# Retention and mixture of experts on one core: the value products of four heads are cut to the key halves their queries see

## The chip, the cores and the metric

The kernel runs on one core of a Trainium2 chip. The metric is the device time of one execution in microseconds (us); three timed runs of the kernel before gave a median of 569.94 us (569.82 to 571.11).

## The reference, cut to what matters

Retention over 8 batches, 8 heads, 576 positions and 64 channels, then a mixture of 16 experts (4 groups of 4) over the 4608 tokens. The change lies in the first part, in `ret @ v`:

```python
B, H, S, D_ = q.shape                        # 8, 8, 576, 64
scores = scale * np.matmul(q, k.transpose(0, 1, 3, 2))
rel = pos[:, None] - pos[None, :]
Dmat = np.where(rel >= 0, gamma[:, None, None] ** rel[None, :, :], 0.0)
ret = scores * Dmat[None, :, :, :]
out = np.matmul(ret, v)                      # causal: a query sees no later key
...
# each token: best group, best expert in it, two layers with ReLU, weighted
ye = np.maximum(xg[mask_e] @ w1[g, e], 0.0) @ w2[g, e]
```

All of the retention is in float32.

## The kernel before, in words

The retention runs over 36 tiles of 128 tokens (`NT`), nine to a pair of batches: eight of one batch each (four tiles per batch) and a ninth (`m` is 1) with the last 64 tokens of both. Earlier tiles of a batch act through a running state, so within a tile only 128 keys by 128 queries are left, masked to be causal. The order on TensorE is written out by hand (the loop at L942): everything there runs in program order, and VectorE, ScalarE, GpSimd and SyncE are pinned to program order too.

In step t of that loop TensorE does, one behind the other: `av(t - 1)` (L887), `state(t)` (L866), `inter(t - 1)` (L902), `scores(t + 1)` (L828), the transposes `xnat_pe(t - 6)` (L427) and, once in three steps each, `logits`, `gate_pe`, `places_pe`.

- `scores` makes keys by queries for eight heads in the PSUM tile `pss` (one buffer, one bank for each `o`). A head is named by s, g and o: h = 4s + 2g + o. From tile 5 on, 64 by 64 products that leave late keys by early queries out (L843) make all heads of two thirds of the tiles and half the heads of the others (t % 3 is 1); the other half there, the second tile of each nine and the first five tiles are made whole (L851).
- `masked` (L856) multiplies `pss` by a mask on VectorE into `sT` (two buffers).
- `av` multiplies `sT` with the scaled values `vs` (three buffers, made by ScalarE in `scale`): for each head 128 keys by 128 queries into the PSUM tile `px`, 64 output rows, so two heads (g = 0, 1) stand side by side in the columns of the array.
- `state` adds the tile's keys by values to the running sums `pst`; `inter` adds, for tiles that have a state before them, state by queries to `px` as 64-row products, four at a time. Eight of the 36 tiles, the first of each batch, have no `inter`; the ninth tiles have two half-wide ones and no `state`.
- `turned` (L919) reads `px` on VectorE into `xT`; what follows (gate, rows to DRAM by GpSimd's scatters, experts) builds on that.

To let 64-row products of two heads stand in different rows of the array, the host exchanges the key halves of every second pair of heads (`_layout`, L1554; the decay constants follow at L1512), so that a head's early keys lie in rows 0 to 63 or 64 to 127. The loads of the tiles (`a`, seven buffers, 1 MB each) go out on SyncE's queue, `loads(t + 6)` in step t. The experts follow on TensorE from step 36 on (L1178).

A float32 product is two MATMUL records on TensorE, a bfloat16 or float32r one is one.

## Time and profile before

| | us |
|---|---|
| median of three runs | 569.94 |
| the profiled execution | 569.17 |
| its span, first to last instruction | 567.4 |
| TensorE busy | 556.8 (98% of the span) |
| VectorE busy | 428.1 (75%) |
| ScalarE busy | 329.8 (58%) |
| granted TensorE clock | 0.999 of full speed |

The span is the stretch that the trace covers; 1.8 us of the execution lie outside it. The retention takes TensorE until 143 us, the experts the rest. In the trace's rows a group such as "PE L894 MATMUL px<-sT,vs 128*64 128x128 f32 x16" is 16 MATMUL records of line 894 that write `px` from `sT` and `vs`; 128*64 are the rows and columns of the array that they use, 128x128 the operand that is streamed (128 partitions, 128 columns).

### The profile page before, as it was taken

The page shows a single profiled execution, that of the slowest core. Times are in us where ns is not written, and L with a number is a line of the kernel's source. Part 1 is how long each engine was busy: PE and PEld are TensorE (multiplying, and loading weights), DVE is VectorE, ACT ScalarE, POOL GpSimd, SP SyncE. Part 2 cuts the span into 40 slices and gives each one's busy share as a digit, 9 for nine tenths or more (in the row PEclk, how much of TensorE's full clock was granted, in tenths as well). Part 3 has the DMA queues.
Part 4 walks back from the last instruction along what each step waited for, and adds up shares of the span by engine and source line. Part 5 has one row for each costly group of instructions (what it writes and reads, how often), then busy time and mean ns, then how long its engine had stood idle before and what let it go on. Part 6 is the DMA issues. An engine that isn't in the chain of part 4 may idle for free.

```text
span 567.4 us, 16419 instructions
## 1 busy us (share of the span) xinstructions
PE 556.8 (98%) x6014; PEld 527.1 (93%) x6014; DVE 428.1 (75%) x1007; ACT 329.8 (58%) x855; POOL 265.3 (47%) x400
## 2 busy tenths in 40 slices
PE   7999999999999999999999999999999999999995
PEld 5888888888799999999999999999999999999994
DVE  5887787878899678876768586777768677687784
ACT  5678878886664545454545455554545455555553
POOL 0022323253502056555564758374564836638564
PEclk9999999999999999999999999999999999999999
DMA  8999999979666975655556464928566484754751
GB/s 334 424 393 344 336 365 333 355 245 353 235 226 276 203 310 154 252 158 243 177 221 209 191 230 183 352 67 335 136 261 210 193 293 143 323 199 195 292 222 42
DMA packets 47639, 142.01 MB, mean 250 GB/s; under 512 B 7825, under 2 KB 28697, under 8 KB 34864
## 3 DMA queue, kind: packets, MB, share of 16 engines
q1 hardware_dynamic: 38176, 120.18, 59.1%
q0 software_dynamic: 9216, 20.34, 9.9%
q8 instruction: 72, 1.18, 0.8%
q14 instruction: 31, 0.25, 0.1%
q10 hardware_dynamic: 144, 0.05, 0.0%
HBM read 120.22 MB, written 24.81 MB: 256 GB/s over the span
## 4 chain that ended last, share of the span: by engine, by line
PE 93%; DMA 2%; POOL 1%; SPq 1%; DVE 1%; issue 1%; ACT 0%; POOLq 0%; ACTq 0%
PE ph L691 35%; PE py L1102 11%; PE py L1104 11%; PE py L1103 11%; PE px L894 6%; PE pxt L434 4%; PE pss L843 3%; PE px L913 3%; PE pst L879 2%; PE py L1091 2%; DMA a<-in_qkv 2%; PE plt L484 2%; PE pss L851 1%; POOL out L121 1%; SPq L121 1%; PE phn L1156 1%
## 5 line engine op out<-in xcount | busy, mean ns | idle before, releaser
L121 POOL DMA_INDIRECT out<-y,ii x151 | 165.4, 1095 | 59.5 <-issue 29.7
L121 DVE TENSOR_TENSOR wl<-r,wh 128x512 fp32r<-128x512 f32 x268 | 172.4, 686 | 4.0 <-ACT wh L121 0.8
L121 ACT ACTIVATE hh<-ph 128x256 fp32r<-128x256 f32 (+15 forms) x128 | 53.8, 420 | 187.5 <-PE ph L691 132.5
L121 ACT CAST wh<-r 128x512 fp32r<-128x512 f32 x268 | 151.6, 618 | 0.0
L691 PE MATMUL ph<-xTh_m,wh 128*128 128x316 f32 (+15 forms) x504 | 148.4, 294 | 0.0
L691 PE MATMUL ph<-xTh_m,wl 128*128 128x316 f32 (+15 forms) x504 | 148.0, 294 | 0.0
L691 PE MATMUL ph<-xTl_m,wh 128*128 128x316 f32 (+15 forms) x504 | 147.9, 294 | 0.0
L1102 PE MATMUL py<-hh,wh 128*128 128x316 f32 (+18 forms) x480 | 142.0, 296 | 0.0
L1104 PE MATMUL py<-hl,wh 128*128 128x316 f32 (+13 forms) x480 | 141.1, 294 | 0.0
L1103 PE MATMUL py<-hh,wl 128*128 128x316 f32 (+13 forms) x480 | 141.0, 294 | 0.0
L121 DVE SCALAR_TENSOR_TENSOR hl<-ph,hh 128x256 fp32r<-128x256 f32 (+14 forms) x126 | 58.5, 464 | 87.0 <-ACT hh L121 86.4
L691 PEld LDWEIGHTS ph<-xTh_m,wh 128*128 128x128 f32 x504 | 95.2, 189 | 0.6 <-issue 0.3
L691 PEld LDWEIGHTS ph<-xTl_m,wh 128*128 128x128 f32 x504 | 95.3, 189 | 0.3
L691 PEld LDWEIGHTS ph<-xTh_m,wl 128*128 128x128 f32 x504 | 95.0, 189 | 0.0
L1104 PEld LDWEIGHTS py<-hl,wh 128*128 128x128 f32 x480 | 90.6, 189 | 0.3 <-DVE hl L121 0.3
L1103 PEld LDWEIGHTS py<-hh,wl 128*128 128x128 f32 x480 | 90.6, 189 | 0.0
L1102 PEld LDWEIGHTS py<-hh,wh 128*128 128x128 f32 x480 | 90.6, 189 | 0.0
L121 POOL COPY pace<-hh 1x1 f32<-1x1 f32 x140 | 35.5, 254 | 117.6 <-ACT hh L121 107.6
L121 ACT ACTIVATE vs<-a,cf 128x64 f32<-128x64 f32 x288 | 72.4, 335 | 7.1 <-DMA a<-in_qkv 6.1
L121 POOL DMA_INDIRECT xs<-xt,sl x33 | 32.7, 990 | 84.0 <-DVE xT L121 33.1
L121 DVE TENSOR_TENSOR sT<-pss,masks 128x512 f32<-128x512 f32 x72 | 46.1, 682 | 9.6 <-PE pss L851 5.1
L894 PE MATMUL px<-sT,vs 128*64 128x128 f32 x576 | 39.9, 279 | 0.5 <-DVE xT L121 0.3
(206 smaller groups left out, 607.7 us busy)
## 6 DMA issues: line engine op xcount, KB each, us to landing
r<-in_w SPq DMA_DIRECT2D x69, 1024.0 KB, 8.1
a<-in_qkv SPq DMA_DIRECT2D x30, 1024.0 KB, 8.6
xb<-xs SPq DMA_DIRECT2D x20, 165.0 KB, 3.8
a<-in_qkv SPq DMA_DIRECT2D x4, 768.0 KB, 6.2
xb<-xs SPq DMA_DIRECT2D x20, 148.5 KB, 3.2
out<-y,ii POOLq DMA_INDIRECT x151, 3.8
xb<-xs SPq DMA_DIRECT2D x12, 181.5 KB, 4.1
xb<-xs SPq DMA_DIRECT2D x12, 132.0 KB, 2.8
```

The lines of the kernel that those rows point to most:

```text
L121: i_ = f(*a, **k)
L434: pe.transpose(T["pxt"][:, i, :], T["xT"][:, i, :], ident)
L484: pe.matmul(plt[32 * i : 32 * i + 32], wgp[:, i, :], tiles[t]["xTg"][:, i], start=True, stop=True)
L691: pe.matmul(ph[:, :w], a[:, kc, cs], b[:, kc, :w], start=n == 0, stop=n == 3 * NKC - 1)
L843: pe.matmul(pss[k_, o, (i + par) * P + late * D : (i + par) * P + to], T["kT"][r, i + par, k_], T["qT"][r, i + par, late * D : to], start= ...
L879: pe.matmul(pst[o * D : o * D + D, i, :], T["k"][:, h, :], T["vs"][:, h, :], start=first and i == 0, stop=True, skip_group_check=True,)
L894: T["av"] = pe.matmul(px[g * D : g * D + D, o, s * P : s * P + P], T["vs"][:, 4 * s + 2 * g + o, :], T["sT"][:, o, 2 * s + g, :], start=s ...
L913: pe.matmul(px[g * D : g * D + D, o, s * P + r * w : s * P + r * w + w], st[rows, 2 * s + g, :], T["qT"][rows, 2 * s + g, r * w : r * w + ...
L1091: pe.matmul(py[:n], a[:, r0 : r0 + n], b[:, f % 2, :], start=st_ and m == 0, stop=sp_ and m == len(ab) - 1,)
L1102: pe.matmul(py[:, :w0], wh[:, f % 2, ds_], hh[:, :w0], start=st_, stop=False)
L1103: pe.matmul(py[:, :w], wl[:, f % 2, ds_], hh[:, :w], start=False, stop=False)
L1104: pe.matmul(py[:, :w], wh[:, f % 2, ds_], hl[:, :w], start=False, stop=sp_)
```

## The change

For the four heads with s = 0, `av` makes the late 64 queries alone (128 keys by 64 queries), and a new function `av_early` makes the early 64 queries from the early 64 keys, as four 64-row products that stand in the four quarters of the array. The loop calls it between `state(t)` and `inter(t - 1)`. The four heads with s = 1 stay as they are. So that the early keys of the two heads o = 0, 1 lie in different rows, the heads whose key halves are exchanged are now those with (s ^ o) = 1 (by constants and by the host's layout); their places in `pss` and `sT` (`turn`) and the order of the 64 by 64 products in `scores` follow, and the mask repeats over the other of the two inner axes.

```diff
+        def turn(o, s, g):
+            return 2 * (s ^ o) + g
         def scores(t):
...
             whole = NP if t < FULL or t % 9 == 1 else part
-            for i in range(0, NP - whole, 2):
+            split = 2 - whole // 2
+            for g in range(split):
                 for late in range(2):
-                    for par in range(2):
+                    for s in range(2):
                         for o in range(2):
-                            k_ = slice((late ^ par) * D, (late ^ par) * D + D)
+                            at = (late ^ s ^ o) * D
+                            k_ = slice(at, at + D)
                             r = slice(o * D, o * D + D)
                             to = late * D + D if T["m"] else P
+                            i = 2 * s + g
+                            at_ = turn(o, s, g) * P
                             pe.matmul(
-                                pss[k_, o, (i + par) * P + late * D : (i + par) * P + to],
-                                T["kT"][r, i + par, k_], T["qT"][r, i + par, late * D : to],
+                                pss[k_, o, at_ + late * D : at_ + to],
+                                T["kT"][r, i, k_], T["qT"][r, i, late * D : to],
...
         def masked(t):
-            mask = masks[:, T["m"]].unsqueeze(1).to_broadcast([P, 2, 2, P])
+            mask = masks[:, T["m"]].unsqueeze(2).to_broadcast([P, 2, 2, P])
...
         def av(t):
             for s in range(2):
+                q0 = 0 if s else D
                 for o in range(2):
                     for g in range(2):
                         T["av"] = pe.matmul(
-                            px[g * D : g * D + D, o, s * P : s * P + P],
-                            T["vs"][:, 4 * s + 2 * g + o, :], T["sT"][:, o, 2 * s + g, :],
+                            px[g * D : g * D + D, o, s * P + q0 : s * P + P],
+                            T["vs"][:, 4 * s + 2 * g + o, :], T["sT"][:, o, turn(o, s, g), q0:P],
                             start=s == 0, stop=True, skip_group_check=True,
                         )
...
+        def av_early(t):
+            T = tiles[t]
+            for g in range(2):
+                for o in range(2):
+                    rows = slice(o * D, o * D + D)
+                    pe.matmul(
+                        T["px"][g * D : g * D + D, o, 0:D],
+                        T["vs"][rows, 2 * g + o, :], T["sT"][rows, o, turn(o, 0, g), 0:D],
+                        start=False, stop=True, skip_group_check=True,
+                    )
...
             if t:
+                av_early(t - 1)
                 inter(t - 1)
...
-            c[:, KC_GK + ci * H + h] = gamma[h] ** -np.roll(pos[ci], h // 2 % 2 * D).astype(np.float64)
+            c[:, KC_GK + ci * H + h] = gamma[h] ** -np.roll(pos[ci], (h // 4 ^ h % 2) * D).astype(np.float64)
...
     for x in nat[1:]:
-        y = x.reshape(NT, P, NP, 2 * D)
-        y[:, :, 1::2] = np.roll(y[:, :, 1::2], D, axis=1)
+        for h in range(H):
+            x[:, :, h] = np.roll(x[:, :, h], (h // 4 ^ h % 2) * D, axis=1)
```

## Rows read from the trace of the kernel before

**Rows 1.** The page: busy time, share and instructions of each engine.
```profile
PE 556.8 (98%) x6014; PEld 527.1 (93%) x6014; DVE 428.1 (75%) x1007; ACT 329.8 (58%) x855; POOL 265.3 (47%) x400
```

**Rows 2.** Windows: stretch, its length, busy time per engine, granted clock, DMA share, GB/s.
```profile
18.00:143.00 125.00, 123.83 (x2684) 104.75 (x2676) 99.78 (x289) 98.47 (x343) 38.51 (x74) 1.00 0.94 348
160.00:560.00 400.00, 400.00 (x3020) 397.55 (x3019) 303.51 (x644) 209.45 (x453) 215.39 (x305) 1.00 0.63 220
```

**Rows 3.** Groups of TensorE by form, first 160 us: records, busy us, mean ns of one.
```profile
L894 PE MATMUL px<-sT,vs 128*64 128x128 f32 x576 | 39.9, 279 | 0.5 <-DVE xT L121 0.3 <-issue 0.3
L879 PE MATMUL pst<-vs,a 128*64 128x64 f32 x512 | 21.1, 223 | 0.1
L913 PE MATMUL px<-a,st 64*64 64x128 f32 x384 | 16.0, 282 | 0.0
L843 PE MATMUL pss<-a 64*64 64x128 f32 x328 | 15.9, 275 | 0.0
...
L843 PE MATMUL pss<-a 64*64 64x64 f32 x456 | 15.0, 218 | 0.3 <-issue 0.3
```

**Rows 4.** Timeline of TensorE in one tile's step: start us, length us, group.
```profile
50.15 1.09 PE L894 MATMUL px<-sT,vs 128*64 128x128 f32 x16
51.08 0.64 PE L879 MATMUL pst<-vs,a 128*64 128x64 f32 x16
51.64 0.67 PE L913 MATMUL px<-a,st 64*64 64x128 f32 x16
52.13 0.51 PE L843 MATMUL pss<-a 64*64 64x128 f32 x16
```

**Rows 5.** Timeline of TensorE, narrow windows: pairs of L894, four at once of L843.
```profile
73.10 0.39 PE L894 MATMUL px<-sT,vs 128*64 128x128 f32 x4
...
67.25 0.64 PE L843 MATMUL pss<-a 64*64 64x64 f32 x32
```

**Rows 6.** Waits of TensorE and its weight loads: us in total, times, longest.
```profile
PE pss L851 <- DMA a<-in_qkv: 1.5, 2, 1.2
...
PEld pst L879 <- ACT st L121: 0.6, 2, 0.3
```

**Rows 7.** Timeline at the start: tiles 4 and 5 scaled, `av(4)` begun.
```profile
18.42 2.02 ACT L121 ACTIVATE vs<-a,cf 128x64 f32<-128x64 f32 x8 [1.95 <-DMA a<-in_qkv]
...
20.85 2.02 ACT L121 ACTIVATE vs<-a,cf 128x64 f32<-128x64 f32 x8 [0.16 <-DMA a<-in_qkv]
...
23.41 1.09 PE L894 MATMUL px<-sT,vs 128*64 128x128 f32 x16
```

**Rows 8.** Loads: all of 1 MB with us to landing; tile 20's issue; its first reader.
```profile
a<-in_qkv SPq DMA_DIRECT2D x30, 1024.0 KB, 8.6
...
59.18 0.33 SPq L121 DMA_DIRECT2D a<-in_qkv  x1
...
77.39 2.01 ACT L121 ACTIVATE vs<-a,cf 128x64 f32<-128x64 f32 x8
```

**Rows 9.** Timeline of a step whose finished tile (13) has no `inter`.
```profile
58.05 1.09 PE L894 MATMUL px<-sT,vs 128*64 128x128 f32 x16
...
58.97 0.63 PE L879 MATMUL pst<-vs,a 128*64 128x64 f32 x16
...
59.19 0.69 DVE L121 TENSOR_TENSOR xT<-px,gq 128x512 f32<-128x512 f32 x1 [1.07 <-PE px L894]
59.53 0.90 PE L843 MATMUL pss<-a 64*64 64x128 f32 x32
...
60.51 1.29 DVE L121 TENSOR_TENSOR sT<-pss,masks 128x512 f32<-128x512 f32 x2 [0.64 <-PE pss L843]
```

**Rows 10.** Waits of VectorE for `px`, and a ScalarE step without idle time before it.
```profile
DVE xT L121 <- PE px L913: 12.4, 14, 2.2
...
79.56 0.68 ACT L121 ACTIVATE xt<-pxt,wt 128x512 f32<-128x512 f32 x1
```

## The prediction

> **What bounds the kernel now.** I read the busy time of each engine first, then the windows, then the waits, then the order of the retention's steps. TensorE is busy for 98% of the span [rows 1]; in the stretch of the retention, 18 to 143 us, for 123.8 of 125 us, and in the experts' for all of 400, at full clock in both [rows 2]. VectorE and ScalarE have some 25 us of the 125 free. Busy alone proves little, since matmuls are pipelined, so I looked for waits: TensorE's largest on a load is 1.5 us in all, and its weight loads lost 0.6 us to ScalarE's copy of the state [rows 6]. And the steps are regular to the hundredth: `av` starts 0.93 us before `state`, that 0.56 before `inter`, that 0.49 before `scores` [rows 4], and this recurs tile after tile. The retention goes as fast as TensorE takes its products, and the experts behind it likewise, so a tenth of a microsecond off each tile's products should come off the end.

> One stretch is excepted. Tiles 4 and 5 are scaled when their loads have landed (ScalarE idles 1.95 and 0.16 us for them [rows 7]); until `state(4)`, behind that first wait, the start goes at the loads' pace, and what `av` saves there is lost. From `av(4)` at 23.41 us [rows 7] on it counts: 32 of 36 tiles. Loads don't bind later. That of tile 20 is issued at 59.18, has landed by about 67.8 with the median of 8.6 us, and is first read at 77.39 [rows 8]: nearly 10 us to spare, against some 3 that TensorE may gain in all.

> **Removed: half the columns of four heads.** Eight heads are 16 records of 128 columns. Two records start side by side (two heads in the array's column halves), so these are eight pairs. Four records that start within one pair's step of each other last 0.39 us together [rows 5], one alone takes 0.273 (the group's mean of 0.279 holds the slower first ones [rows 3]): a step of 0.11 us per pair. As a control, eight steps of 0.11 and 0.05 more for the first (its second weights aren't in yet) make 0.93, the distance from `av` to `state` [rows 4]. For 64 columns I take `state`: it uses the same 128 by 64 of the array, the same weights' shape and streams 64 columns. Its 16 records last 0.64 us, one 0.223 [rows 3, 4], so the last pair starts 0.42 behind the first: seven steps of 0.059. Four pairs go from 0.109 to 0.059: 0.20 us off a tile (0.23 if a step of 128 columns is taken as the 0.82 us between first and last start, in seven steps).

> **Added: `av_early`.** Four products of 64 rows, 64 weight columns and 64 streamed columns: eight records, in two rounds of four. The trace has just that form, the 64 by 64 scores: 32 records last 0.64 us and one 0.218 [rows 3, 5], so eight rounds have a step of 0.060. Two rounds cost 0.12 us. The first step after a change of array shape is longer by some 0.05 (0.49 us for `inter`'s four rounds of 128 columns, where four steps of 0.11 are 0.44 [rows 4]); `av_early` takes this over from the `inter` behind it, or in the eight tiles without one from the `scores` behind it, which are of the same shape, so it is not paid twice.

> What I weighed against this is the change of shape itself. From `state` to `inter` the array goes from 128 rows to 64: the last pair of `state` starts 0.42 us behind its first, and `inter` 0.14 behind that [rows 4], where a step alone is 0.06. So a change costs about 0.08 us, nearly what a tile is to gain. [...] Here the call stands between `state` and a group of 64-row products, so the number of changes stays.

> **Moved at no cost.** `scores` has as many products of the same forms; their order within four, and the place of each in `pss`, differ. `masked` has the same two instructions on as many elements, the mask only repeating over the other axis. The exchange of halves is in constants and the input's layout; the loads keep bytes and order. `sT` and `vs` are read a little longer: the buffer of `sT` is written again by `masked(t + 1)`, which waits for `scores(t + 1)` anyway, behind `av_early` on TensorE; `vs` has three buffers. The load that waits on `av` of a batch's first tile waits on the same product (its last is one of s = 1).

> One wait is longer: in a tile without `inter`, `turned` now waits for `av_early`, behind `state`, instead of `av`. In tile 13 VectorE begins it at 59.19, and ends at 59.88; `scores` behind it let `masked` start only at 60.51, after 0.64 us of idling [rows 9]. `av_early` would end about 0.5 us later than `av` did, so `turned` ends near 60.4, with `scores` no earlier than that. The 0.64 us cover it; without that cover the mask would start up to 0.2 us late in seven tiles, 1.4 us in all if TensorE felt every one.

> **The sum.** 0.20 less 0.12 is 0.08 a tile by rounded steps, 0.11 by the coarser one, bounds of 0.075 and 0.11; I take 0.09, nearer the clean pairs. Times 32 it is 2.9 us (2.4 to 3.5). TensorE is all there is in the chain, the copies on the other engines follow it, so the profiled execution goes from 569.17 to 566.3, its span from 567.4 to 564.5. The median of the runs before is 0.8 above the profiled execution, so as a median: 569.9 less 2.9, 567.0.

> **Rivals.** *The gain is given back.* ScalarE and VectorE each fill four fifths of the stretch [rows 2], and ScalarE has steps without any idle time before its copy of `pxt` [rows 10]; its late copy of the state already held TensorE up twice [rows 6]. If a step of 0.09 us less makes this frequent, half or more of the gain turns into such waits: 568.5 to 569.9. Against it: VectorE waits 12.4 us for `inter`'s products [rows 10], so it follows rather than leads, and ScalarE's 98.5 us leave 0.8 us of each tile's 3.7 idle, nine times what is taken.

> [...]

> *Slower: the 64 by 64 scores lose their overlap.* Before, the four products of a round take the quarters of the array column by column; after, the second shares neither rows nor columns with the first. If the two records of a product then ran in an order that fills two quarters only, each round would take two steps. There are 82 rounds of 128 columns (328 records) and 114 of 64 (456) [rows 3]: 82 by 0.11 and 114 by 0.06 are 15.8 us, less the 2.9: 582.8. It decides once a fifth of the rounds is hit. Against it: the quarters work side by side now in two orders (the late half begins with the other column), and each stretch of four still has four different quarters. Nothing in this trace shows the diagonal order.

> **How the numbers follow.** About 0.3%, 1.7 us, is what a measurement of this kernel can tell from no change. The forecast 0.78; given back 0.14; weight loads 0.03; overlap lost 0.05. The forecast's 2.4 to 3.5 us and the scatter of the runs make 566.0 to 568.2, and to hold the time 8 times in 10 the range takes in the larger part of the second case, to 569.4. Faster is the forecast, a gain that lies between 2.4 us and the bound included: 0.78; same is the second case: 0.14; slower the last two: 0.08.

> **What would show it.** `av` should start 0.72 us before `state`, not 0.93; `av_early` should put eight records and 0.11 to 0.12 us between `state` and `inter`; L843's 32 records should keep their length, but last 0.85 instead of 0.90 us [rows 9] behind a tile without `inter`; the experts should begin about 2.9 us earlier with the same durations. [...] A start of the experts that is earlier with the end unmoved would mean that I misjudged what bounds them.

## The result: slower, although every product costs what the sum said

| | before | after |
|---|---|---|
| median of 20 runs each, us | 570.42 (568.39 to 574.3) | 575.35 (569.88 to 581.79) |
| ratio | | 1.0069, 95% interval 1.0046 to 1.0091 |
| profiled execution, us | 569.17 | 575.72 |
| its span, us | 567.4 | 573.9 |
| first product of line 691, in the experts, us | 151.85 | 158.88 |
| from there to the last product, us | 408.8 | 408.4 |

The kernel became 0.7% slower where 2.9 us less were forecast: 4.9 us between the medians of the table, 3.9 us between the means (570.57 and 574.49) of the executions that the ratio uses. The ratios leave out executions over 1.5% above the fastest of their kernel as slow, here three of the changed kernel's 20 (579.83 to 581.79 us, at a granted clock of 0.989 to 0.990) and one of e9_filler_before's six (1132.97 us).

The first product of line 691, before and after:

```profile
151.85 0.37 PE L691 MATMUL ph<-xTh_m,wh 128*128 128x256 f32 x1
...
158.88 0.36 PE L691 MATMUL ph<-xTh_m,wh 128*128 128x256 f32 x1
```

From there on the experts take as long as before; all of it is lost ahead of them, in the retention. Yet the steps there are as short as forecast. The timeline of TensorE in one step of the changed kernel (start us, length us, group; L905 is `av`, L889 `state`, L919 `av_early`, L936 `inter`, L851 the split scores), then a step whose finished tile has no `inter`:

```profile
55.90 0.64 PE L889 MATMUL pst<-vs,a 128*64 128x64 f32 x16
56.46 0.34 PE L919 MATMUL px<-sT,vs 64*64 64x64 f32 x8
56.63 0.62 PE L936 MATMUL px<-a,st 64*64 64x128 f32 x16
57.06 0.85 PE L851 MATMUL pss<-a 64*64 64x128 f32 x32
...
59.21 0.89 PE L905 MATMUL px<-sT,vs 128*64 128x64 f32 x16
59.93 0.64 PE L889 MATMUL pst<-vs,a 128*64 128x64 f32 x16
60.50 0.34 PE L919 MATMUL px<-sT,vs 64*64 64x64 f32 x8
60.66 0.85 PE L851 MATMUL pss<-a 64*64 64x128 f32 x32
```

`av` starts 0.72 us before `state` (0.93 in [rows 4]); `av_early` puts 0.17 us in front of `inter`, and `inter` takes 0.43 to 0.44 instead of 0.49. That is 0.09 us less per tile. The scores with their new order last 0.85 us as in the tile of before that followed an `inter`, and 0.85 instead of 0.90 behind a tile without one [rows 9]. The one of before that followed an `inter`:

```profile
47.97 0.67 PE L913 MATMUL px<-a,st 64*64 64x128 f32 x16
48.46 0.85 PE L843 MATMUL pss<-a 64*64 64x128 f32 x32
```

The same stretch of the windows as in [rows 2], and two more of the changed kernel (stretch, its length, busy time per engine with instructions, granted clock, DMA share, GB/s):

```profile
18.00:143.00 125.00, 118.74 (x2863) 100.12 (x2863) 95.61 (x266) 95.19 (x333) 35.88 (x67) 0.99 0.90 330
95.66:102.32 6.66, 5.16 (x128) 4.53 (x128) 5.03 (x16) 4.41 (x17) 1.92 (x5) 1.00 0.89 304
102.40:105.80 3.40, 3.40 (x33) 3.05 (x35) 1.80 (x5) 1.56 (x6) 0.27 (x2) 0.51 0.69 285
160.00:560.00 400.00, 400.00 (x3031) 398.24 (x3030) 303.63 (x649) 209.37 (x452) 212.07 (x303) 1.00 0.64 223
```

TensorE has 6.3 us of idle time in the 125 us, where it had 1.2, and in one stretch, 102.4 to 105.8, a granted clock of 0.51, where before it was 1.00 over all of the 125 us [rows 2]. Its waits (who waited for what, us in total, times, longest) say that nothing in the profile held it:

```profile
PE pss L851 <- issue: 3.4, 5, 1.0
PE pss L861 <- issue: 1.5, 1, 1.5
PE px L936 <- issue: 1.1, 2, 0.7
```

In the kernel before, the same view shows three such waits, and much shorter:

```profile
PE pss L843 <- issue: 0.3, 1, 0.3
PE px L894 <- issue: 0.3, 1, 0.3
PE pxt L434 <- issue: 0.2, 1, 0.2
```

### The profile page after: what moved, and what is told of

Read it like the earlier page. It is cut to its first block, busy times and chain, and to the rows that moved or that the text cites. A ratio compares the mean times of both kernels' runs of the same rounds, so it can differ in the third digit from the quotient of the medians.

```text
span 573.9 us, 16995 instructions
## 1 busy us (share of the span) xinstructions
PE 559.5 (97%) x6302; PEld 528.7 (92%) x6302; DVE 429.0 (75%) x1007; ACT 330.2 (58%) x855; POOL 264.3 (46%) x400
## 4 chain that ended last, share of the span: by engine, by line
PE 96%; issue 2%; POOL 1%; DMA 1%; DVE 0%; POOLq 0%; DVEq 0%
PE ph L691 35%; PE py L1126 11%; PE py L1127 11%; PE py L1128 11%; PE px L905 5%; PE pxt L434 4%; PE pss L851 3%; PE pss L861 3%; PE pst L889 3%; PE py L1115 2%; PE px L936 2%; PE px L919 2%; PE plt L484 2%; POOL out L121 1%; PE phn L1180 1%
## 5 line engine op out<-in xcount | busy, mean ns | idle before, releaser
L691 PE MATMUL ph<-xTh_m,wh 128*128 128x316 f32 (+15 forms) x504 | 148.2, 294 | 0.0
L691 PE MATMUL ph<-xTl_m,wh 128*128 128x316 f32 (+15 forms) x504 | 147.7, 293 | 0.0
L691 PE MATMUL ph<-xTh_m,wl 128*128 128x316 f32 (+15 forms) x504 | 147.7, 293 | 0.0
L691 PEld LDWEIGHTS ph<-xTh_m,wh 128*128 128x128 f32 x504 | 95.0, 188 | 0.6 <-issue 0.3
L691 PEld LDWEIGHTS ph<-xTl_m,wh 128*128 128x128 f32 x504 | 95.1, 189 | 0.3
L691 PEld LDWEIGHTS ph<-xTh_m,wl 128*128 128x128 f32 x504 | 94.9, 188 | 0.0
L121 DVE TENSOR_TENSOR xT<-px,gq 128x512 f32<-128x512 f32 x36 | 24.7, 686 | 20.9 <-PE px L936 13.0
```

The costliest lines, as they stand in the source:

```text
L121: i_ = f(*a, **k)
L691: pe.matmul(ph[:, :w], a[:, kc, cs], b[:, kc, :w], start=n == 0, stop=n == 3 * NKC - 1)
```

## Where the idle time lies

The waits fall in the middle of groups. The longest of the changed kernel, in the timeline of TensorE:

```profile
100.11 0.71 PE L861 MATMUL pss<-a 64*128 64x128 f32 x6
102.32 0.50 PE L861 MATMUL pss<-a 64*128 64x128 f32 x1 [1.50 <-issue]
```

Six of the eight records that make four heads' scores whole run, then nothing for 1.5 us, then the rest. All eight read one tile's load, so nothing that they need came in between. So I counted TensorE's records from the start, LDWEIGHTS, MATMUL and semaphore records alike. The gaps of over half a microsecond in the retention, behind its first 20 us, stand before records 961, 1217, 1730, 3009, 3522, 4290, 4802 and 6081; the three of the kernel before stand before 1218, 1473 and 3266. All of these are one number (193 to 195) modulo 256. In the windows above, 95.66 to 102.32 us is one such stretch: 128 MATMULs and 128 LDWEIGHTS.

The trace also has the DMA packets that bring instructions. In that stretch one of 16384 bytes moves on the instruction queue q8, between 99.98 and 100.98 us. The packets of this 1 us window by queue (queue, kind: packets, MB, share of the 16 engines):

```profile
q0 software_dynamic: 60, 0.21, 56.1%
q1 hardware_dynamic: 14, 0.09, 24.0%
q8 instruction: 1, 0.02, 6.2%
```

Theory: a block of 256 instructions must last longer than its successor takes to arrive (the time until its packet starts, 0.9 us of transfer, 1.3 us until TensorE goes on). The change adds 16 instructions a tile and makes the tile shorter, so blocks run out sooner. By the blocks between 20 us and the last 15 us of the retention, without the gaps, a block lasted 5.81 us before and lasts 5.29 now; a packet starts 2.68 and 2.92 us after TensorE entered the block, 1.1 to 4.3 us in single cases. On the mean, then, a block still arrives in time (some 4.9 us against 5.81, and 5.1 against 5.29); it is the packets that start late that leave a gap. Rivals that I tested: the new order of the scores or the exchange makes the gaps; the cut of `av`, its short pairs, does; the 64-row products of `av_early` do.

## The experiments

For all of them: the idle time at block ends is the sum, over the retention, of what the gap at the end of each block of 256 exceeds 0.11 us by, an ordinary step of TensorE.

| kernel | time against before, 95% interval | TensorE's instructions ahead of the first expert product | block lasts, us | packet starts after, us | idle at block ends, us | first expert product, us |
|---|---|---|---|---|---|---|
| before | 1 | 5918 | 5.81 | 2.68 | 1.8 | 151.85 |
| after | 1.0069 (1.0046 to 1.0091) | 6494 | 5.29 | 2.92 | 8.3 | 158.88 |
| e1_exchange | 0.998 (0.9956 to 1.0003) | 5918 | 5.82 | 2.56 | 1.7 | 151.66 |
| e2_records | 1.0111 (1.0052 to 1.017) | 6494 | 5.46 | 2.54 | 4.1 | 157.79 |
| e5_halves | one execution | 5918 | 5.66 | 2.85 | 6.8 | 152.75 |
| e7_copies | 1.0038 (1.0007 to 1.007) | 5918 | 5.86 | 3.44 | 4.7 | 155.73 |
| e3_paced_before | 1.0045 (1.002 to 1.0069) | 5944 | 5.81 | 3.14 | 5.0 | 155.83 |
| e4_paced_after | 1.014 (1.0105 to 1.0176) | 6520 | 5.25 | 3.20 | 9.7 | 159.94 |
| e8_filler | 1.0309 (1.0276 to 1.0342) | 6782 | 5.83 | 1.57 | 0.9 | 169.55 |
| e9_filler_before | 1.0333 (1.0291 to 1.0375) | 6206 | 6.43 | 1.64 | 0.9 | 174.18 |
| e10_filler_after | 1.0297 (1.0255 to 1.0338) | 6782 | 5.83 | 1.91 | 0.7 | 169.10 |
| e11_fewer | 1.0081 (1.0054 to 1.0107) | 5710 | 6.64 | 2.14 | 0.8 | 160.69 |

**The exchange alone.** `av` whole again, `av_early` not called, all else as in the change:

```diff
-                q0 = 0 if s else D
+                q0 = 0
...
-                av_early(t - 1)
```

> The change without its cut: the heads' key halves are exchanged the new way, pss and sT have the new places and the scores the diagonal order, but av makes all 128 columns of all heads and av_early is not called. As many TensorE instructions as before. Theory (TensorE's instructions arrive in blocks of 256, and the change asks for them faster than the DMA brings them): as the kernel before, 569.5 to 571.5 us, first expert product (L691) near 152 us, idle gaps at block ends some 2 us in all. Rival (the diagonal order of the 64 by 64 scores, or the exchange, costs the time): 573 to 577 us, and longer groups of L851 or gaps in them.

Measured: 0.998 of before, the first expert product at 151.66 us, 1.7 us idle at block ends. The exchange and the diagonal order of the scores cost nothing; my rival of lost overlap falls. Its one gap of over half a microsecond stands before record 2753, a block end again, and its packet ended 1.3 us earlier, though the profile puts it down to ScalarE:

```profile
71.53 0.60 PE L434 MATMUL pxt<-cf,xT 128*128 128x128 f32 x4 [1.13 <-ACT vs L121]
```

So such a wait need not carry the name "issue"; its place tells.

**More instructions, no column less.** The kernel before with four spare products in front of `inter`:

```diff
+        def spare(t):
+            T = tiles[t]
+            for g in range(2):
+                for o in range(2):
+                    rows = slice(o * D, o * D + D)
+                    pe.matmul(
+                        T["px"][g * D : g * D + D, o, 2 * P : 2 * P + D],
+                        T["vs"][rows, 2 * g + o, :], T["sT"][rows, o, g, 0:D],
+                        start=False, stop=True, skip_group_check=True,
+                    )
...
+                spare(t - 1)
                 inter(t - 1)
```

> The kernel before with four spare 64 by 64 products of 64 columns per tile in front of inter, into columns of px that nobody reads: 16 instructions more per tile, as in the change, no column less. The products themselves cost 36 by 0.116, 4.2 us. Theory (instruction supply): gaps at block ends grow from 1.8 us to some 4 or 5, so 576 to 580 us. Rival (the cut of av's columns, its short pairs, makes the gaps): 574 to 575.5 us with gaps as before.

Measured: 576.1 us, 1.0111 of before. Idle time at block ends went from 1.8 to 4.1, at the low end of what was expected. Its waits of TensorE on nothing that the profile shows:

```profile
PE pl L497 <- issue: 1.2, 1, 1.2
PE px L925 <- issue: 1.1, 2, 0.8
...
PE pss L843 <- issue: 0.7, 1, 0.7
```

One of them stands before `pl`, the transposes of the gate, between two 128 by 128 products: the place in the stream of instructions decides, not the kind of product. The gaps stand before records 961, 1217, 2498 and 4802, again the same modulo 256. The products' 4.2 us and 2.3 us of idle time make 6.5; the first expert product comes 5.9 us later.

**Fewer columns, no more instructions.** The change without its call of `av_early`, with `px` one tile that is cleared once:

```diff
-            px = ps_x.tile([P, 2, 4 * P], F32, name=f"px_{t}", tag="x")
...
-                av_early(t - 1)
```

> The change without av_early: the early queries of four heads lack what their own tile gives (left out of the computation, so the experts get other rows, and only the retention is to be compared; px is one tile that is cleared once). No added instruction, 0.20 us less per tile. Theory (instruction supply): blocks run some 0.3 us shorter than before, so gaps grow to some 3 to 5 us, fewer than in the change; first L691 product between 146 and 149 us. Rival (the 64-row products between state and inter make the gaps): no more gaps than before, 145 us.

Measured in one execution: 6.8 us idle at block ends, where 3 to 5 were expected, and one of the gaps, at 41.6 us, of 2.5 us, followed by 3.4 us at a granted clock of 0.50. Its longest wait and the stretch behind it:

```profile
PE px L906 <- issue: 2.3, 1, 2.3
...
45.00:48.40 3.40, 3.40 (x49) 2.49 (x49) 1.81 (x3) 0.67 (x2) 0.99 (x1) 0.50 0.86 250
```

The first expert product comes at 152.75 us, 0.9 later than before: of the 6.4 us that 32 tiles save, the gaps took 5.0 and the clock 1.7 (an estimate, half of the 3.4 us), and 0.6 more have no place that I can name. The expected 146 to 149 was missed: the gaps were longer than I thought, and I had not counted that the clock could fall behind a long one, as it did here. There is no `av_early` here, so it isn't its products that make the gaps; shorter blocks do it as well as more instructions.

**More DMA traffic.** First a quarter of each load sent twice to the same place:

```diff
+                if t >= RB:
+                    sp.dma_start(a[:, 0:1], qkv[t, :, 0:1])
                 i_ = sp.dma_start(a[:, 0:n], qkv[t, :, 0:n])
```

> The kernel before with a quarter of every load from tile 7 on sent twice (256 KB more per tile); its result and TensorE's work are the same. Theory (instruction blocks wait in the DMA engines behind the loads): packets of instructions start later, gaps at block ends grow from 1.8 us to 5 or more, 573 to 580 us, with the loads still ahead of their readers. Rival (loads have 10 us to spare and instructions don't care): 569.5 to 571.5 us.

Measured: 631.72 us, 1.1074 of before (1.1028 to 1.112), and no test of the theory: TensorE waits 43.9 us for loads in all, against 1.5 before [rows 6]. That the second transfer waits for the first to land, so that loads no longer overlap, is how I explain it, from the edit; it isn't shown. Its largest wait and the stretch of the windows:

```profile
PE pss L845 <- DMA a<-in_qkv: 34.8, 18, 2.7
...
18.00:143.00 125.00, 93.55 (x1953) 76.86 (x1949) 70.30 (x190) 70.20 (x247) 23.34 (x41) 0.97 0.75 271
```

One thing it shows beside the point: with the DMA engines 75% busy instead of 94%, packets of instructions started 1.0 us after TensorE entered the block on the mean instead of 2.7. Then a copy within DRAM that nothing waits for:

```diff
                 i_ = sp.dma_start(a[:, 0:n], qkv[t, :, 0:n])
+                if t >= RB:
+                    scr = dp.tile([P, DM // 2], F32, name=f"scr_{t}")
+                    sp.dma_start(scr, qkv[t, :, 0, 0 : DM // 2])
```

> The kernel before with 128 KB per tile, from tile 7 on, copied within DRAM behind each load: a tenth more DMA traffic that nobody waits for; its result and TensorE's work are the same. Theory (instruction blocks wait behind the DMA traffic): gaps at block ends grow from 1.8 us to 3 to 7, 571.5 to 577 us. Rival (instructions don't care): 569.5 to 571.5 us.

Measured: 574.12 us, 1.0038 of before (1.0007 to 1.007). The windows' stretch and its waits on nothing that the profile shows:

```profile
18.00:143.00 125.00, 121.16 (x2621) 101.99 (x2613) 96.83 (x274) 96.13 (x335) 37.02 (x69) 1.00 0.97 369
...
PE pss L846 <- issue: 1.8, 4, 0.7
```

TensorE's instructions are those of before. The copies add bytes (369 GB/s instead of 348 [rows 2]) and packets (12623 in the 125 us instead of 8677); with them the packets of instructions start 0.8 us later, and idle time at block ends goes from 1.8 to 4.7 us. So in this kernel the arrival hangs on the DMA traffic; whether on its bytes or on the number of its packets, this run doesn't tell.

**Loads in two halves.** Half of each load waits for `av` of the next step:

```diff
-                i_ = sp.dma_start(a[:, 0:n], qkv[t, :, 0:n])
+                h_ = 2 if t >= LOADS - 1 else n
+                i_ = sp.dma_start(a[:, 0:h_], qkv[t, :, 0:h_])
+                T["rest"] = a[:, h_:n], qkv[t, :, h_:n]
...
+        def rest(t):
+            if t < NT:
+                i_ = sp.dma_start(*tiles[t]["rest"])      # waits for tiles[t - LOADS + 1]["av"]
...
                 av(t - 1)
+                rest(t + LOADS - 2)
```

> The kernel before with each load from tile 6 on in two halves: the second goes out half a step later, behind av, so that less lies in the DMA engines at a time. Same bytes, same work on TensorE. Theory (instruction blocks wait behind the loads): the gaps at block ends, 1.8 us, shrink to under 1; 569 to 571 us. Rival (the gaps have nothing to do with the loads): the same gaps, 570 to 571.5.

> The changed kernel with its loads in two halves in the same way. Theory (instruction blocks wait behind the loads): packets of instructions start earlier on the mean than 2.8 us behind the request, gaps shrink from 8.3 us to 2 to 5, the time to 568 to 573 us. Rival (the gaps come from the number of instructions alone, or from TensorE itself): 574 to 577 us as the change.

Both expectations failed, and so did both rivals: both kernels became slower than either had it (1.0045 and 1.014 of before). The packets of instructions did not start earlier but later, 3.1 and 3.2 us after TensorE entered the block, and idle time grew with that, to 5.0 and 9.7 us. The link from delay to idle time held; my idea of how to shorten the delay did not. The loads now move in smaller packets (12317 of 12765 in the 125 us of e3_paced_before are under 8 KB, before 4798 of 8677), half as many again. Whether that or the moment of the halves makes the delay wasn't separated.

**Blocks that last longer.** Four cheap products per tile behind `av`, into columns that nobody reads:

```diff
             T["px"] = px
+            for i in range(4):
+                pe.matmul(
+                    px[:, i % 2, 2 * P : 4 * P], ones, ones.unsqueeze(1).to_broadcast([P, 2, P]),
+                    start=False, stop=True, skip_group_check=True,
+                )
```

> The changed kernel with four bfloat16 products of 256 columns more per tile, into columns that nobody reads: 0.43 us of TensorE time for only 8 instructions, so a block of 256 instructions lasts longer. The products cost 36 by 0.43 to 0.48, 15.5 to 17 us. Theory (a block's instructions must last longer than its successor takes to arrive): the gaps go back to 1 to 3 us and no stretch at half the clock behind them, so 583 to 587 us, less than the sum. Rival (the gaps are the early products' own): 590 to 593 us, the full sum.

Measured: 587.37 us, between the two ranges; the idle time at block ends, 0.9 us, decides for the theory, and there is no stretch at half the clock in the retention (1.00 over the 125 us). My price of the filler, an estimate, was too low: by this run's trace it costs 0.70 us a tile (0.54 for itself and its way to `state`, 0.15 for the longer starts of the groups around it), 25 us for 36 tiles. By the ratios the time rose by 13.7. Part of the rest is the start, where loads set the pace (TensorE waits 2.2 us for them in this run); the gaps' 7.4 us are the other large part. A longer tile also thins the DMA traffic (307 GB/s instead of 330), and the packets start 1.3 us earlier.

With the filler in both kernels, on one chip:

> The kernel before with the same four bfloat16 filler products per tile as the changed kernel had in the run before (0.70 us a tile with the changes of shape that they bring, by that run's trace). Theory (once blocks of instructions arrive in time, the cut is worth what its products are): no gaps over 1 us in all, and 2 to 3.5 us slower than the changed kernel with the filler, which is some 590 us. Rival (the cut brings nothing even then): equal to it within 1 us.

> The changed kernel with the filler once more, on the same chip as the kernel before with the filler. Theory: about 587 us as in its first run, 2 to 3.5 us below the kernel before with the filler. Rival: equal to that one within 1 us.

Measured: 589.84 us without the change, as the median of five executions, and 586.59 with it, both with under 1 us idle at block ends. The windows' stretch of the latter, TensorE busy throughout:

```profile
18.00:143.00 125.00, 125.00 (x2770) 98.15 (x2773) 86.96 (x241) 89.15 (x312) 33.62 (x63) 1.00 0.85 307
```

Between the medians lie 3.3 us, by the ratios to the kernel before 2.1, with intervals that overlap, so the times alone don't settle it. The traces do. `av` of tile 12 and of tile 30, first without the change, then with it:

```profile
61.21 1.09 PE L894 MATMUL px<-sT,vs 128*64 128x128 f32 x16
140.10 1.09 PE L894 MATMUL px<-sT,vs 128*64 128x128 f32 x16
...
58.23 0.89 PE L905 MATMUL px<-sT,vs 128*64 128x64 f32 x16
135.55 0.89 PE L905 MATMUL px<-sT,vs 128*64 128x64 f32 x16
```

The 18 tiles take 78.89 and 77.32 us, 0.087 us less for each. Once instructions arrive in time, the change is a gain of the size that the sum gave.

**Fewer instructions, more work.** The changed kernel with all scores whole:

```diff
-            whole = NP if t < FULL or t % 9 == 1 else part
+            whole = NP
```

> The changed kernel with the scores of all tiles made whole: 32 instructions less in 21 tiles and 16 less in 10, about 830 of the retention's 6200, for more TensorE time: by the change's trace 0.31 us a tile where all heads were split, and 0.11 for one more change of shape in most tiles, some 10 us in all. Theory (instruction supply): gaps at block ends fall from 8.3 us to under 1.5 and no half clock follows one, so the time stays near the change's, 573 to 578 us, though TensorE has 10 us more to do. Rival (the early products or the cut make the gaps): 583 to 587 us.

Measured: 581.81 us in a session in which the kernel before takes 577.72, a ratio of 1.0081; the change itself has 1.0069. With the expected times divided by 570.4, the theory's were 1.005 to 1.013 and the rival's 1.022 to 1.029. Idle time at block ends is 0.8 us. (There are 784 instructions less, not 830: seven tiles had half their heads split, not ten.) TensorE has some 10 us more to do in the retention, and the kernel takes about as long as the change; it is faster than neither. Two of its waits on "issue" do not stand at a block end:

```profile
PE px L936 <- issue: 0.9, 2, 0.5
```

They come in the middle of a block, and what ended them isn't known.

## Why the prediction was wrong

*The terms of the products were right.* Four pairs off: `av` starts 0.72 us ahead of `state`, as forecast. `av_early` costs 0.17 us, of which `inter` or the scores give back 0.05, so 0.116; the sum's 0.09 us per tile is what the steps show. The scores and the experts kept their durations, and no change of array shape was added.

*The step that failed is the price of what was added, and the sentence under the sum that TensorE is all there is in the chain.* I priced `av_early` by the time of its eight MATMULs and did not price its 16 instructions. That the kernel before had its three gaps of half a microsecond 256 records apart could be seen in its trace; its waits on "issue", 0.3, 0.3 and 0.2 us, were too small for me to look at, and I took the regular steps as proof that nothing else was near the limit. They did not recur without exception: across the block end at 66.5 us `state` took 0.86 us,

```profile
65.97 0.86 PE L879 MATMUL pst<-vs,a 128*64 128x64 f32 x16
66.76 0.67 PE L913 MATMUL px<-a,st 64*64 64x128 f32 x16
```

and where they did, a block of 5.81 us was only just enough for a next one that comes after 4.9 us on the mean and after some 6.4 at the latest (4.2, 0.9 and 1.3). From there the gain could not be had: each tenth of a microsecond off the tile shortens the block, and each instruction more does so again.

*The account.* The first expert product comes 7.0 us later. The products are 2.8 us shorter. Idle time at block ends is 6.5 us more. The 3.4 us at a clock of 0.51 behind the longest gap I put at 1.7, half their length (16 records of L905 last 1.55 us there, 0.89 in the step above). The start is 1.0 us later (by the block that begins at 12.07 us before and at 13.05 now; in this execution the clock came to full speed at 13.7 us, before at 6.5, as the whole scores' 16 records show, with 2.08 us at 8.63 and 1.16 at 16.61, before 1.88 at 4.95 and 1.16 at 8.64; which is no matter of the change: six later kernels built on it came to full speed at 4.0 to 5.3 us). That makes 6.4; 0.6 us have no place that I can name. This is the account of one execution of each, 6.5 us apart, and not of the medians. How much the lower clock costs in the others isn't known. Their mean granted clocks hint that it is no single case: 0.995 or less in 14 of the changed kernel's 20 executions, the profiled one with 0.994 among them, and in 9 of 60 of the kernel before in the sessions of the experiments.

*The rivals.* That the gain is given back to waits was the right kind, at the wrong place and with the wrong size: I looked to ScalarE and VectorE, and bounded it at the time of before. That the weight loads would set the pace of `av`'s short products, for which I gave 0.03, would have left `av` at 0.93 before `state`; no run shows it, and the trace has 0.72. Lost overlap of the scores: refuted by L851's lengths and e1_exchange. The longer wait of `turned` came out tighter than forecast: behind a tile without `inter`, VectorE now goes from `xT` to the mask without idling,

```profile
60.91 0.69 DVE L121 TENSOR_TENSOR xT<-px,gq 128x512 f32<-128x512 f32 x1 [1.63 <-PE px L919]
61.59 1.29 DVE L121 TENSOR_TENSOR sT<-pss,masks 128x512 f32<-128x512 f32 x2
```

with the scores done at 61.51 (60.66 and 0.85). The 0.64 us of cover [rows 9] are all used, and 0.08 us more; TensorE shows no wait for it.

*The range.* It was built on product times and their bounds alone, so the cost of supplying instructions lay outside any case; the rivals that made the kernel slower had other causes, which the runs refute. The low end of the runs after lies at 569.88 and the median at 575.35, against 566.0 to 569.4.

## What to carry to other kernels

In this kernel instructions had a price beside that of their work: in e2_records 16 more per tile took the idle time at block ends from 1.8 to 4.1 us. On an engine that takes over 40 of them per microsecond, as here (5360 in the 125 us), count instructions per 256 and compare how long a block lasts (5.81 us before, 5.29 now) with how long the next one takes to arrive under the kernel's own DMA traffic (some 4.9 and 5.1 on the mean). Small idle times that fall in the middle of groups, with "issue" as what ended them, are worth a look at their places: count the records between two of them, and look for the packet that ended just before. Not every such wait is one (two in e11_fewer are not), and one can stand under another engine's name (as in e1_exchange). The edit made TensorE's work shorter by cutting it into more products, and that paid where blocks lasted 5.83 us (0.087 us a tile, with the filler), not where they lasted 5.29: there 16 instructions a tile bought 0.09 us and cost more than that.

## What the runs showed of the hardware

I had not expected TensorE to run out of instructions in a stretch without branches: the trace's first branch record of TensorE comes at 169.8 us before and at 176.8 now, behind all the gaps above. In the kernels before and after, a block of 256 arrives 1.1 to 4.3 us plus 0.9 after TensorE has entered the block before it, and where there is a gap, TensorE goes on 1.2 to 1.6 us after the packet's end. Over these runs the delay before the packet starts is longer with more traffic on the core's DMA engines, though not strictly with the bytes: on the mean it is 1.0 us at 271 GB/s, 1.6 and 1.9 at 307, 2.7 at 348 and 3.4 at 369, but 2.9 at the changed kernel's 330, and 2.1 and 3.2 at 327 in e11_fewer and e4_paced_after. Over all the runs it is 1.0 to 1.9 us with 6500 to 8000 DMA packets in the 125 us, 2.1 to 2.9 with 8200 to 8700, and 3.1 to 3.4 with over 12500; which of the two counts wasn't separated. And one gap cost more than its length: behind the idle gap of 1.8 us before 102.32 the granted clock was 0.51 for 3.4 us, while the gaps of up to 1.3 us in the same execution left it at 1.00. The gap of 2.5 us in e5_halves was followed by the same fall (0.50 for 3.4 us); gaps of 1.6 and 1.7 us in e3_paced_before and e4_paced_after were not (1.00 over the 125 us).
